# Emitting the engine programs without a Block, with the final waits shared between ScalarE and SyncE

## The chip, the cores and the metric

The kernel runs on one core of a Trainium2 chip. The metric is the device time of one execution in microseconds (us). The core has five engines that run their own instruction streams and meet only at semaphores: TensorE (PE in the profile), VectorE (DVE), ScalarE (ACT), GpSimd (POOL) and SyncE (SP), which here only issues transfers (DMAs) and waits.

## What is computed

One input `x` of 2048 tokens by 640 features is normalised, and two branches of the normalised `xn` are added to it: a linear attention with 32 heads of 20 features, and a dense layer with GELU.

```python
def _A_ref(x, wqkv, wo):
    H = 32; Dh = D // H
    qkv = (x @ wqkv).reshape(B, S, 3, H, Dh).transpose(2, 0, 3, 1, 4)
    q, k, v = qkv[0], qkv[1], qkv[2]
    phi = lambda t: jnp.where(t > 0, t + 1, jnp.exp(t)) + 1e-6
    pq, pk = phi(q), phi(k)
    kv = jnp.einsum("bhsd,bhse->bhde", pk, v)
    z = jnp.einsum("bhsd->bhd", pk)
    num = jnp.einsum("bhqd,bhde->bhqe", pq, kv)
    den = jnp.einsum("bhqd,bhd->bhq", pq, z)[..., None] + 1e-6
    return (num / den).transpose(0, 2, 1, 3).reshape(B, S, D) @ wo

def _B_ref(x, w1, b1, w2, b2):
    return jnp.einsum("bsf,fd->bsd", _gelu(jnp.einsum("bsd,df->bsf", x, w1) + b1), w2) + b2

xn = _layernorm(x, axis=-1)
return x + _A_ref(xn, A_wqkv, A_wo) + _B_ref(xn, B_w1, B_b1, B_w2, B_b2)
```

All inputs and the output are bf16; F, the width of the dense layer, is 1536.

## The kernel before

The 2048 tokens are cut into 16 tiles of 128 (`t`), in 4 chunks of 4 (`c`). In order of time, TensorE does this: transposes and the first dense layer (lines 382 and 352) with GELU on ScalarE; the keys of all tiles (line 473); the product of `phi(k)` with `xn`, summed over all tokens (line 512); the queries (line 524), with the small products that fold values and `wo` into one matrix `Msb` (lines 533 and 551) and the denominators (line 562) among them; and then, per token tile, the second dense layer and the attention's output in one accumulation (line 615). The last tile is done in three column parts of 320, 192 and 128 (line 651).

VectorE adds the residual to each finished tile (line 634; the last tile's parts at line 654) and writes a small buffer `out_sb`. SyncE then issues the store to the output (line 637; parts at line 657). In the same last stage SyncE also copies the reciprocals of the denominators to all partitions (`rden_dma`, line 586: four transfers for each of four chunks). ScalarE has no work in that stage after the five copies into `Msb` at line 556, and GpSimd none after the memset at line 480.

The order of the work is written out by hand. A small class `Planner` records it: `ins` appends an instruction to the list of its engine with the semaphore values that it has to wait for, and remembers per engine what has already been waited for. Each DMA has a semaphore of its own, complete at 16. `wait_event` appends a record that has waits and no instruction. `emit` goes through the five lists, in the order TensorE, VectorE, ScalarE, GpSimd, SyncE, and puts out every wait (line 94) ahead of its instruction; waits that are left at the end of a list go out at line 108.

At the end (lines 683 to 692) the kernel before lets SyncE wait for the last three records of its own list, which are the stores of the three parts, and emits each engine's list into a block of its own inside `nc.Block()`. Closing that block emits the instructions that the profile has at line 691: a drain on every engine, then a barrier in which GpSimd collects the other four and releases them. An opening barrier, line 706, comes with the making of the program and is no part of the block.

The head of the kernel is touched only in that it too is no longer inside a block. There SyncE loads the tokens and most of the weights (lines 229 and 233), and ScalarE, ahead of its first activation (line 392, with a load of the activation table), issues two loads (line 233): the bias `b1` and the first quarter of `W1`, which TensorE needs at line 382.

Of the kernel before, what the change touches and what calls it, by code (L numbers as in the profile page):

```python
# [23 lines left out]
class Planner:  # L24
# [55 lines left out]
    def emit(self, block):  # L80
        nc = self.nc
        for idx, eng_name in enumerate(ENGINES):
            recs = self.records[eng_name]
            if not recs:
                continue

            def body(eng, recs=recs, eng_name=eng_name):
                pending_waits = []
                for (waits, fns, ev, dma) in recs:
                    pending_waits.extend(waits)  # L90
                    if not fns:
                        continue
                    for (key, val) in pending_waits:
                        eng.wait_ge(self.sems[key], val)
                    pending_waits = []
                    ins = None
                    for fn in fns:
                        r = fn(eng)
                        if r is not None:
                            ins = r  # L100
                    if ev is not None:
                        key, val = ev
                        if dma:
                            ins.then_inc(self.sems[key], 16)
                        else:
                            ins.then_inc(self.sems[eng_name], 1)
                for (key, val) in pending_waits:
                    eng.wait_ge(self.sems[key], val)

            getattr(block, eng_name)(body)  # L110


def bass_parallel_sum__linear_attn_block__dense_activation_gelu__prompt_kernel(
# [16 lines left out]
    Pl = Planner(nc)  # L130
# [6 lines left out]
    with contextlib.ExitStack() as es:  # L137
# [45 lines left out]
        def take(n):  # L183
            b = ring[0]
            if n == 2 and b % 2:
                b += 1
            b %= 8
            ring[0] = (b + n) % 8
            return b
# [278 lines left out]
        for t in range(NT):  # L468
            b = take(2)
            fns = []  # L470
# [142 lines left out]
        def mm(b, t, i, h):  # L613
            l, r = mm_ops(t, i)
            return lambda e: e.matmul(bank(b + h, 0, HW), l, r[:, h * HW:(h + 1) * HW],  # L615
                                      start=(i == 0), stop=(i == JT + DT - 1))

        def mm_reads(t, i):
            return [r_HG[t][i], r_W2] if i < JT else [r_PQ[t // CH][i - JT]] + r_M[i - JT]

        def out_w2(t, lo=0, hi=JT, b=None):
            b = take(2) if b is None else b
            for i in range(lo, hi):
                Pl.ins("tensor", [mm(b, t, i, 0), mm(b, t, i, 1)], reads=mm_reads(t, i), writes=B_[b:b + 2],
                       mark=(i == JT - 1))
            return b
# [13 lines left out]
        def out_last(t):  # L640
            xb(t)
            lo = 0
            for i, w in enumerate((HW, 3 * 64, P)):
# [5 lines left out]
                for q in range(JT + DT):  # L649
# [7 lines left out]
                Pl.ins("sync", lambda e, hs=hs, o=o: e.dma_start(ov[t * P:(t + 1) * P, hs], o),  # L657
                       reads=[r_out3 if i == 2 else r_out[i]], dma=True)

        bs = [out_w2(0)]  # L660
        bs += [(bs[0] + 2 * i) % 8 for i in range(1, 4)]
        m_step(bs[1:4])
# [17 lines left out]
                rden_dma({4: 2, 7: 3}[t])  # L680
        out_last(NT - 1)

        for (waits, fns, ev, dma) in Pl.records["sync"][-3:]:
            Pl.wait_event("sync", ev)

        with contextlib.ExitStack() as ses:
            for e_ in ENGINES:
                Pl.sems[e_] = ses.enter_context(nc.semaphore(f"s_{e_}"))
            for i in range(Pl.ndma):
                Pl.sems[f"dma{i}"] = ses.enter_context(nc.semaphore(f"s_dma{i}"))  # L690
            with nc.allow_low_precision("bf16 operands as in the reference"), nc.Block() as block:
                Pl.emit(block)


# [26 lines left out]
```

## Time and profile before

| | |
|---|---|
| median of three timed runs | 209.23 us (209.12 to 209.23) |
| the profiled execution, its own time | 208.79 us |
| its span, first to last instruction of the program | 207.0 us |
| TensorE busy | 203.1 us (98%) |
| VectorE, ScalarE, GpSimd busy | 112.3, 73.2, 21.2 us |
| output stores of a whole tile, issue to landing | 1.8 us |
| stores of the last three parts, issue to landing | 1.6, 1.5, 1.4 us |
| clock granted to TensorE | 1.00 |

The span counts everything that the program itself issues, waits and barriers among it. Waits, barriers, branches and the issuing of transfers are done by an engine's sequencer and are not counted as busy. They carry a "q" behind the engine's name (SPq, POOLq; PEld is TensorE's loading of weights). A transfer's time to landing runs from its issue to the arrival of its semaphore. The profiled execution is one, and its own time lies somewhat below the median of the timed runs.

### The profile page before, as it was taken

The numbers are of one execution on the slowest core, as the hardware profiler recorded it, in microseconds if no ns is written. First come the engines' busy times: TensorE is split into PE (matmuls) and PEld (weight loads), VectorE is DVE, ScalarE is ACT, GpSimd is POOL, SyncE is SP. The second block draws the span as 40 slices with busy tenths as digits, with TensorE's granted clock in tenths as the row PEclk, the third lists the DMA queues.
The fourth block names the chain that finished last, engine by engine and source line by source line (L and its number), as shares of the span: only waits on it lengthen the run. The fifth ranks groups of instructions, "written<-read, shape, count | busy, mean of one in ns | idle before, by whom it ended". The sixth has DMA issues, their size and how long they took to land.

```text
span 207.0 us, 3957 instructions
## 1 busy us (share of the span) xinstructions
PE 203.1 (98%) x1588; PEld 140.4 (68%) x1588; DVE 112.3 (54%) x231; ACT 73.2 (35%) x141; POOL 21.2 (10%) x59
## 2 busy tenths in 40 slices
PE   7999999999999999999999999999999999999995
PEld 2799987444457777777756556777777777777775
DVE  4589970000007888999298887564863422523322
ACT  2689887666676455111153553400000000000000
POOL 3235568000031000000000000000000000000000
DMA  6999678997000000000300001921212111001001
GB/s 180 345 354 103 106 131 149 372 324 263 3 0 0 0 0 3 0 3 0 63 0 5 0 0 48 375 96 44 88 42 69 53 38 54 32 32 36 32 33 62
DMA packets 24042, 18.31 MB, mean 88 GB/s; under 512 B 10584, under 2 KB 24024, under 8 KB 24024
## 3 DMA queue, kind: packets, MB, share of 16 engines
q1 hardware_dynamic: 23344, 17.57, 29.8%
q10 hardware_dynamic: 680, 0.49, 0.8%
q8 instruction: 12, 0.20, 0.4%
q14 instruction: 6, 0.05, 0.1%
HBM read 12.62 MB, written 2.62 MB: 74 GB/s over the span
## 4 chain that ended last, share of the span: by engine, by line
PE 96%; DMA 3%; ACTq 0%; DVE 0%; issue 0%
PE ps L615 34%; PE ps L352 25%; PE ps L512 10%; PE ps L473 10%; PE ps L524 10%; DMA W<-in_B_w_dram 3%; PE ps L651 2%; PE ps L551 1%; PE ps L533 1%; PE ps L562 1%; PE ps L382 0%; PE ps L336 0%; ACTq L233 0%; DVE out_sb L654 0%
## 5 line engine op out<-in xcount | busy, mean ns | idle before, releaser
L352 PE MATMUL ps<-xnT,W 128*128 128x128 bf16 (+2 forms) x435 | 52.0, 282 | 0.0
L615 PE MATMUL ps<-W,HG 128*128 128x320 bf16 x360 | 51.0, 299 | 0.0
L352 PEld LDWEIGHTS ps<-xnT,W 128*128 128x128 bf16 x435 | 35.6, 98 | 15.6
L615 PEld LDWEIGHTS ps<-W,HG 128*128 128x128 bf16 x360 | 35.1, 98 | 14.2 <-issue 0.4
L356 ACT ACTIVATE HG<-ps,b1c 128x128 bf16<-128x128 f32 (+2 forms) x87 | 40.0, 493 | 12.4 <-PE ps L352 10.3
L460 ACT ACTIVATE ek<-ps 128x512 bf16<-128x512 f32 (+1 forms) x36 | 23.2, 645 | 20.3 <-PE ps L524 10.6
L634 DVE TENSOR_TENSOR out_sb<-ps,xnT 128x640 bf16<-128x640 f32 x15 | 12.4, 825 | 33.1 <-PE ps L615 32.9
L461 DVE TENSOR_SCALAR ek<-ek 128x512 bf16<-128x512 bf16 (+1 forms) x36 | 10.9, 303 | 33.7 <-ACT ek L460 32.5
L615 PE MATMUL ps<-Msb,PQ 128*128 128x320 bf16 x150 | 22.3, 299 | 0.0
L524 PE MATMUL ps<-xnT,Wqkv 128*128 128x512 bf16 x100 | 21.9, 379 | 0.0
L473 PE MATMUL ps<-Wqkv,xnT 128*128 128x320 bf16 x160 | 21.9, 299 | 0.0
L512 PE MATMUL ps<-xPK,xn_tm 128*128 128x320 bf16 x160 | 21.9, 299 | 0.0
L473 PEld LDWEIGHTS ps<-Wqkv,xnT 128*128 128x128 bf16 x160 | 15.7, 98 | 6.2
L512 PEld LDWEIGHTS ps<-xPK,xn_tm 128*128 128x128 bf16 x160 | 15.7, 98 | 6.1
L615 PEld LDWEIGHTS ps<-Msb,PQ 128*128 128x128 bf16 x150 | 14.7, 98 | 5.7
L524 PEld LDWEIGHTS ps<-xnT,Wqkv 128*128 128x128 bf16 x100 | 11.7, 117 | 9.5
L463 DVE SCALAR_TENSOR_TENSOR PQ<-ps,ek 128x512 bf16<-128x512 f32 x20 | 13.8, 692 | 2.1
L308 DVE BATCH_NORM_STATS2 stats<-xPK 128x6 f32<-128x320 bf16 x32 | 13.6, 466 | 2.4 <-DMA xPK<-in_A_x_dram 2.3
L463 DVE SCALAR_TENSOR_TENSOR xPK<-ps,ek 128x640 bf16<-128x640 f32 x16 | 13.2, 825 | 1.7
L499 DVE TENSOR_TENSOR Msb<-Msb,xPK 128x640 f32<-128x640 f32 x14 | 11.6, 825 | 0.5
L318 POOL TENSOR_TENSOR rstd<-aggr,mhalf 128x1 f32<-128x1 f32 x16 | 9.1, 569 | 8.9 <-DVE aggr L316 8.9
L516 ACT ACTIVATE W<-ps 128x640 bf16<-128x640 f32 x5 | 3.5, 705 | 18.2 <-PE ps L512 18.2
(61 smaller groups left out, 93.6 us busy)
## 6 DMA issues: line engine op xcount, KB each, us to landing
xnT<-in_A_x_dram SPq DMA_DIRECT2D x4, 640.0 KB, 6.2
Wqkv<-in_A_wqkv_dram SPq DMA_DIRECT2D x3, 800.0 KB, 6.5
out_dram<-out_sb SPq DMA_DIRECT2D x15, 160.0 KB, 1.8
W<-in_B_w_dram SPq DMA_DIRECT2D x1, 1920.0 KB, 15.9
W<-in_B_w_dram SPq DMA_DIRECT2D x3, 480.0 KB, 7.0
xPK<-in_A_x_dram SPq DMA_DIRECT2D x2, 640.0 KB, 8.7
Wo<-in_A_wo_dram SPq DMA_DIRECT2D x1, 800.0 KB, 11.3
xPK<-in_A_x_dram SPq DMA_DIRECT2D x4, 160.0 KB, 4.2
```

Source lines behind the costliest of these rows:

```text
L308: Pl.ins(v, lambda e: e.bn_stats(stats[:, s, 6 * h:6 * h + 6], x_in[:, t, h * HW:(h + 1) * HW]), reads=[r_x[t]], writes=[r_stats[s][h]])
L352: Pl.ins("tensor", [(lambda e, k=k: e.matmul(bank(b, 0, w), W1[:, k, jb * P:(jb + 1) * P], xnT[:, k, tok], start=(k == 0), stop=(k == DT - ...
L356: Pl.ins("scalar", lambda e: e.activation(HG[:, jb, tok], bank(b, 0, w), ACT.Gelu_apprx_tanh, bias=b1c[:, jb:jb + 1]), reads=[B_[b], r_b1c ...
L460: Pl.ins("scalar", lambda e: e.activation(e2, src, ACT.Exp), reads=br, writes=[r_ek[s]])
L461: Pl.ins(v, lambda e: e.tensor_scalar(et, et, 1.0, 1e-6, ALU.min, ALU.add), reads=[r_ek[s]], writes=[r_ek[s]])
L463: Pl.ins(v, lambda e: e.scalar_tensor_tensor(out=d2, in0=src, scalar=0.0, in1=e2, op0=ALU.max, op1=ALU.add), reads=br + [r_ek[s]], writes= ...
L473: fns.append(lambda e, k=k, h=h, b=b, t=t: e.matmul(bank(b + h, 0, HW), xnT[:, k, t * P:(t + 1) * P], Wqkv[:, k, D + h * HW:D + (h + 1) * ...
L499: Pl.ins(v, lambda e, t=t: e.tensor_tensor(out=zsum, in0=zsum, in1=PK[:, t, :], op=ALU.add), reads=[r_PK[t], r_zsum], writes=[r_zsum])
L512: Pl.ins("tensor", [(lambda e, t=t, h=h, b=b, f=f: e.matmul(bank(b + h, 0, HW), xn_tm[:, t, f * P:(f + 1) * P], PK[:, t, h * HW:(h + 1) * ...
L524: Pl.ins("tensor", [(lambda e, k=k, j=j, b=b: e.matmul(bank(b), Wqkv[:, k, j:D:DT], xnT[:, k, cc], start=(k == 0), stop=(k == DT - 1))) fo ...
L615: return lambda e: e.matmul(bank(b + h, 0, HW), l, r[:, h * HW:(h + 1) * HW], start=(i == 0), stop=(i == JT + DT - 1))
L634: Pl.ins(v, lambda e: e.tensor_tensor(out=halves(out_sb[:, s, :]), in0=pair(b), in1=halves(x_res[:, t, :]), op=ALU.add), reads=B_[b:b + 2] ...
```

## The change

The engine lists are emitted one after the other straight into the main program, where before each went into a block. `nc.Block()` and what its closing emits are gone. The final waits are other ones: all DMAs that SyncE issues from `n_sync` on, which is set after the queries and the four reloads of `x`, are gathered in `stores` (the copies of `rden`, the stores of 15 tiles and of the three parts). ScalarE waits for all of these but the last, at the end of its own list; SyncE waits for the last one.

```diff
@@ emit
-            getattr(block, eng_name)(body)
+            body(getattr(nc, eng_name))
@@ kernel function
+        n_sync = len(Pl.records["sync"])
         bs = [out_w2(0)]
...
         out_last(NT - 1)
 
-        for (waits, fns, ev, dma) in Pl.records["sync"][-3:]:
-            Pl.wait_event("sync", ev)
+        stores = [ev for (waits, fns, ev, dma) in Pl.records["sync"][n_sync:] if dma]
+        for ev in stores[:-1]:
+            Pl.wait_event("scalar", ev)
+        Pl.wait_event("sync", stores[-1])
...
-            with nc.allow_low_precision("bf16 operands as in the reference"), nc.Block() as block:
-                Pl.emit(block)
+            with nc.allow_low_precision("bf16 operands as in the reference"):
+                Pl.emit(None)
```

## The prediction

> **What bounds the kernel now.** I read the page's first line and busy shares, then the chain that ended last, then its end in order of time, then SyncE's own waits, and last every instruction of the closing barrier (line 691).
>
> The page and its chain:
> ```profile
> span 207.0 us, 3957 instructions
> PE 203.1 (98%) x1588; PEld 140.4 (68%) x1588; DVE 112.3 (54%) x231; ACT 73.2 (35%) x141; POOL 21.2 (10%) x59
> ...
> PE 96%; DMA 3%; ACTq 0%; DVE 0%; issue 0%
> ```
> TensorE is busy in 98% of the span and carries 96% of the chain. Nothing this diff touches lies in that stretch. The other 3% is one transfer at the start, the first quarter of W1. The chain in order of time has it, and the end:
> ```profile
> 0.80 0.62 ACTq L233
> 1.42 0.04 issue
> 1.45 5.34 DMA W<-in_B_w_dram
> ...
> 6.83 1.01 PE ps L382 x15
> ...
> 200.09 4.67 PE ps L651 x51
> 204.77 0.02 issue
> 204.79 0.29 DVE out_sb L654
> ```
> The chain counts compute only and stops at 204.79 + 0.29 = 205.08 us; the span goes on to 207.03. So 1.95 us of the span lie behind the last compute instruction: the last store, and the program's end. SyncE's own waits and the closing barrier's instructions show them:
> ```profile
> SPq L108 <- DMA out_dram<-out_sb: 1.1, 1, 1.1
> ...
> SPq L691 <- PEq L691: 0.2, 1, 0.2
> ```
> ```profile
> L691 POOLq EVENT_SEMAPHORE  x2: 17/17/17, 206.8 to 206.9; - x2
> ...
> L691 PEldq DRAIN  x1: 1222/1222/1222, 203.6 to 203.6; - x1
> L691 DVEq DRAIN  x1: 330/330/330, 204.8 to 204.8; - x1
> L691 SPq COMPARE_BRANCH  x1: 41/41/41, 206.6 to 206.6; - x1
> L691 SPq DRAIN  x1: 13/13/13, 206.8 to 206.8; - x1
> L691 SPq EVENT_SEMAPHORE  x1: 17/17/17, 207.0 to 207.0; - x1
> ...
> L691 PEldq EVENT_SEMAPHORE  x1: 51/51/51, 207.0 to 207.0; - x1
> ```
> The view rounds starts to 0.1 us; the trace's records hold nanoseconds. By them the last store is issued at 205.112 and lands at 206.554. SyncE's wait for two of the three stores (line 108) runs 206.571 to 206.599, the branch that leaves its block and carries the third wait 206.636 to 206.677, its drain 206.809 to 206.822, GpSimd collects at 206.847 and releases at 206.930 to 206.947, and the engines leave between 206.971 (SyncE) and 207.034 (TensorE, 51 ns). The end is bound by the last store and then by 207.034 - 206.554 = 0.48 us of waiting and barrier.
>
> **What the Trainium skill says.** (1) "Runtime: NRT & Kernel Launch", section "The ~15µs preamble/postamble breakdown": the runtime puts its own barrier behind the kernel, about 1.5 us that wait for all engines, and a hop of such a chain through the engines costs 44 ns. The profile shows nothing of this: the run took 208.79 us against a span of 207.03, and the 1.76 us outside carry no label. They are less than the sum of the page's stages, so only part of these can be in the time. (2) The same page, "Instruction fetch mechanics": a taken branch whose target isn't in the current window forces a fetch. SyncE's branch is followed by a hole of 206.809 - 206.677 = 0.132 us ahead of its drain, against 0.037 us between its wait and the branch; it fits, without showing the cause. (3) "Perfetto Trace Analysis", section "DMA Instruction — HWDGE (DVE, Sync)": a transfer's semaphore comes after its write is confirmed, which can take surprisingly long to HBM. The trace agrees: 32 KB take 1.44 us from issue to landing, and the change leaves that wait where it is.
>
> **The change, part by part.**
>
> *The end on SyncE.* Removed: the branch with its fetch hole, the drain, the two GpSimd steps and the five releases. Kept: one wait for the last store. I take it at the row of line 108, starting 17 ns behind the landing and taking 28 ns: 206.571 to 206.599. The three waits become one, but the first two had been satisfied at 204.996 and 205.716, so only the third ever counted. The span should end at 206.60: a gain of 207.034 - 206.599 = 0.435 us. Bounds: at most 0.48, if the wait itself cost nothing; at least 0.435 - 0.078 - 0.145 = 0.21 us, if a branch and a drain of the same cost still follow the wait (206.599 to 206.677, then 206.677 to 206.822).
>
> *The other engines' ends.* Their drains go too. TensorE's runs over the last matmuls, DVE's over the last add, ScalarE's is done at 133.42 and GpSimd's at 63.15; all are over by 205.14, 1.4 us ahead of the landing. Worth nothing: the store covers them, and were that cover gone DVE's 0.33 us would be the price.
>
> *ScalarE's new waits.* `stores` holds every DMA that SyncE issues after `n_sync`: 16 copies of rden (line 586), 15 output stores (line 637) and 3 parts (line 657), 34 in all. ScalarE waits for the first 33. Its last activation ends at 133.38 and nothing of it is queued behind the waits, so they hold up nobody; no engine waits for ScalarE after line 556. A wait instruction on ScalarE takes 17 to 38 ns (line 94), so even 33 of them, with the 0.06 us gap SyncE shows between such waits, come to 33 x 0.10 = 3.3 us of its 73 us of idleness. They are met as the stores land, in the order of issue. The last is for the second part, landed at 205.716; with one more wait of 0.1 us ScalarE is through at about 205.82, and SyncE only at 206.60. Cost nothing, with 0.78 us to spare; without that cover, the last wait's 0.1 us.
>
> *The start.* No branch into a block is recorded: from the opening barrier (line 706) to the first work are 0.066 us on SyncE and 0.056 on ScalarE, and 0.058 between SyncE's first two transfers. The gain is between 0 and 0.03 us; I take 0. No DMA changes its queue or place, and no buffer comes free at another time.
>
> *Behind the span.* Before, all five engines leave within 63 ns of each other. After, four have left long ago when SyncE ends, and may have done their share of the runtime's barrier. The trace shows none of it. One bound is 0; the other an estimate from the runtime page: of a chain up and down five engines the four hops up can be done ahead, 4 x 0.044 = 0.18 us. I take the middle, 0.09.
>
> *Sum.* Against the profiled execution: 208.79 - 0.435 - 0.09 = 208.27 us. The three timed runs have a median of 209.23, 0.44 longer than that execution; none of the terms depends on what sets them apart, so from the median: 209.23 - 0.53 = 208.70 us. TensorE is what is late next: it ends at 204.77, and add, store and landing follow.
>
> **The rivals.** *R1, the forecast:* the barrier goes and nothing replaces it, 208.70, with 208.54 (0.48 + 0.03 + 0.18 gained) to 208.80 (0.435 gained) for its own bounds apart from noise. For it: every step removed stands behind the last landing in the records.
>
> *R2, something takes its place.* The main program ends with a branch and drain of its own (gain 0.21 and no more, 209.02), or what follows outside the span has a start-up of its own on SyncE, a fetch for instance, which the 0.48 us used to hide (gain near 0, up to 209.23). For it: 1.76 us outside the span that no record explains, and a hole of 0.13 us at the only branch. Against it: SyncE did not reach its end early before; its fetch could run ahead of the barrier only by the last 0.48 us. I put it at 209.08, between its two forms.
>
> *R3, slower: ScalarE's first load is issued later.* W1's first quarter goes out on ScalarE's queue at 1.452, after b1, and holds TensorE until 6.83. The activation table load of line 392 (1.283 us) stands behind that issue now. If the straight program put it ahead, W1 would land 1.28 us later; PE is nearly gapless from there, so all of it would reach the end: 209.23 + 1.28 - 0.53 = 209.98. It decides from 0.53 us of delay, where it eats the gain. Against it: the table load has the line of the first activation and stands just before it though the block begins two issues earlier, so it goes with the activation and not with the block's head.
>
> **How the numbers follow.** About 0.2% (0.42 us) is what a measurement of this kernel can tell from no change. R1's middle, a gain of 0.53, is only just beyond it; its low bound, 0.435, sits on it, so noise can carry it to either side. R1 has 0.68, of which 0.58 fall faster and 0.10 same. R2 has 0.22: 0.21 same, 0.01 slower by noise. R3 and other shifts at the start have 0.10, slower. So faster 0.58, same 0.31, slower 0.11. The timed runs differ by 0.11 us, and the profiled one by 0.44, so the range has to reach past R1's own: down to 208.35, R1's best with a little of that spread, and up to 209.20, which takes in nearly all of R2 and leaves out R3. R1's own range with the noise is 208.40 to 208.95.
>
> **What would show it.** Right: no record of line 691 at all, SyncE's last instruction a wait that starts some 17 ns after the last landing and ends the span, about 1.5 us behind the last add; ScalarE with some 17 to 33 waits after 133.4, the last before 206; first matmul of line 382 still at 6.8; time outside the span 1.7 us. Wrong: a branch or drain behind SyncE's wait, or an outside part of over 2.1 us (R2); a table load ahead of ScalarE's first transfers and line 382 later than 7.3 (R3). If the outside part is the same to 0.02 us, the 0.09 was nothing and the gain is 0.44.

## The result and the profile after

The changed kernel takes 208.17 us (median of six runs, 207.96 to 208.50) against 209.18 us for the kernel before (six runs, 208.82 to 209.55). The ratio is 0.9953 with a 95% interval of 0.9940 to 0.9967: faster by 0.5%, or 1.01 us by the medians. The forecast was 208.70, a gain of 0.53, and its range reached down to 208.35.

First, the kernel after: the page's first two lines, and SyncE's own waits from 195 us on (who waited for whom, us in total, times, longest).

```profile
span 206.8 us, 3962 instructions
PE 203.2 (98%) x1588; PEld 140.3 (68%) x1588; DVE 112.3 (54%) x231; ACT 73.1 (35%) x141; POOL 21.1 (10%) x59
```
```profile
SPq L637 <- DVE out_sb L634: 8.5, 2, 4.3
SPq L657 <- DVE out_sb L654: 3.1, 3, 2.1
SPq L108 <- DMA out_dram<-out_sb: 1.1, 1, 1.1
```

The wait for the barrier (line 691) is gone; the wait for the last store stands as it did, 1.1 us. The waits at line 108 in the kernel after (engine, operation, count; shortest, median and longest in ns; first and last start):

```profile
L108 ACTq EVENT_SEMAPHORE  x17: 17/38/38, 159.1 to 205.9; - x17
L108 SPq EVENT_SEMAPHORE  x1: 17/17/17, 206.8 to 206.8; - x1
```

ScalarE's 33 waits became 17 instructions. The last starts at 205.935, and SyncE's wait runs from 206.750 to 206.767 and ends the span. The last store lands at 206.733, so from landing to the end of the span it is now 0.034 us, where it was 0.480: 0.45 us gained there. The chain of the kernel after, its start and its end:

```profile
1.45 5.37 DMA W<-in_B_w_dram
...
6.87 1.01 PE ps L382 x15
...
8.16 3.65 PE ps L352 x55
11.82 0.37 PE ps L336 x5
...
200.28 4.67 PE ps L651 x51
204.95 0.02 issue
204.97 0.29 DVE out_sb L654
```

The start is as it was: W1's first quarter goes out at 1.45 and TensorE takes it up at 6.87. In this one execution the last compute lies 0.18 us later than in the one before (204.97 against 204.79): 0.04 from line 382's start, 0.09 from the five transposes at 11.82, 0.05 from the matmuls ahead of them. All of that lies in the first 12 us, where TensorE still depends on loads: the transposes wait 0.20 us for `xn_tm` there, and VectorE, ahead of making it, waited 0.65 us for a load of tokens where it had waited 0.44. Such differences come without any change to the head of the program: in the profiled executions of the experiments below, line 382 starts anywhere from 6.58 to 7.47 us at the full granted clock. The span is therefore only 207.034 - 206.767 = 0.27 us shorter (0.45 - 0.18).

The rest is outside. The profiled execution took 208.04 us, so 208.04 - 206.767 = 1.27 us lie outside its span, against 1.76 before. Over the six runs after, the difference of time and span (spans to 0.1 us) is 1.20 to 1.28 us, median 1.24. Some six tenths of the gain (0.48 of 0.75 us between the two profiled executions) are in time that no instruction of the program occupies. No record shows how this time is divided between what lies ahead of the span's first instruction and what lies behind its last. That the end is what differs follows only from the experiments, where kernels that differ in their final waits alone differ outside.

### The profile page after: what moved, and what is told of

It is laid out like the page before. It is cut to its first block, busy times and chain, and to the rows that moved or that the text cites. A ratio compares the mean times of both kernels' runs of the same rounds, so it can differ in the third digit from the quotient of the medians.

```text
span 206.8 us, 3962 instructions
## 1 busy us (share of the span) xinstructions
PE 203.2 (98%) x1588; PEld 140.3 (68%) x1588; DVE 112.3 (54%) x231; ACT 73.1 (35%) x141; POOL 21.1 (10%) x59
## 4 chain that ended last, share of the span: by engine, by line
PE 96%; DMA 3%; ACTq 0%; DVE 0%; issue 0%
PE ps L615 34%; PE ps L352 25%; PE ps L473 11%; PE ps L512 11%; PE ps L524 10%; DMA W<-in_B_w_dram 3%; PE ps L651 2%; PE ps L551 1%; PE ps L533 1%; PE ps L562 1%; PE ps L382 0%; PE ps L336 0%; ACTq L233 0%; DVE out_sb L654 0%
```

## The experiments

All kernels give the whole computation. Each was timed over several executions with the kernel before on the same chip. "Outside" is time less span, as a median over the kernel's timed executions; "landing to end" is, in the profiled one, its time less the moment, counted from the span's start, at which the last store lands. Both leave out the start, whose differences blur the whole times. The kernel before was measured again with each group (e1 to e4, e5, e6): 209.32, 209.31 and 209.27 us, outside 1.90, 1.95 and 1.89 (lowest 1.70, highest 2.08). The table's row for it has the time of the result and the outside part of the last group. Two of the profiled executions (e3_straight_barrier and e5_last_pe) had a granted clock of 0.992 and are 2 us longer than the medians of their kernels; of them only what follows the last landing is used.

| kernel | us | ratio to before (95%) | outside | landing to end |
|---|---|---|---|---|
| before | 209.18 | | 1.89 | 2.24 |
| after | 208.17 | 0.9953 (0.9940 to 0.9967) | 1.24 | 1.31 |
| e1_straight_old_waits | 208.37 | 0.9955 (0.9938 to 0.9973) | 1.30 | 1.36 |
| e2_block_new_waits | 209.11 | 0.9990 (0.9971 to 1.0009) | 1.74 | 2.13 |
| e3_straight_barrier | 208.85 | 0.9985 (0.9973 to 0.9998) | 1.74 | 2.02 |
| e4_all_wait_last | 208.79 | 0.9982 (0.9963 to 1.0001) | 1.73 | 1.85 |
| e5_last_pe | 208.46 | 0.9958 (0.9942 to 0.9973) | 1.57 | 1.64 |
| e5_last_dve | 208.44 | 0.9967 (0.9937 to 0.9997) | 1.39 | 1.45 |
| e5_last_act | 208.40 | 0.9959 (0.9949 to 0.9969) | 1.59 | 1.57 |
| e5_last_pool | 208.73 | 0.9970 (0.9961 to 0.9980) | 1.83 | 1.88 |
| e6_block_both_waits | 209.06 | 0.9988 (0.9969 to 1.0007) | 1.74 | 2.23 |
| e6_all_but_pool | 208.62 | 0.9967 (0.9953 to 0.9982) | 1.52 | 1.61 |
| e6_pool_second | 208.15 | 0.9942 (0.9923 to 0.9962) | 1.26 | 1.31 |
| e6_pool_part_late | 208.47 | 0.9955 (0.9942 to 0.9969) | 1.57 | 1.56 |

### Blocks, barrier or waits

*e1_straight_old_waits.* The straight program with the old final waits:
```diff
-        for ev in stores[:-1]:
-            Pl.wait_event("scalar", ev)
-        Pl.wait_event("sync", stores[-1])
+        for (waits, fns, ev, dma) in Pl.records["sync"][-3:]:
+            Pl.wait_event("sync", ev)
```


> The straight program, but with the final waits of before: SyncE waits for the three parts' stores, ScalarE for nothing. The time outside the span was 1.76 us before and 1.24 after. Theory A (four engines that leave early do their share of what follows ahead of SyncE, so it is the arrival together that costs): outside 1.2 to 1.3 us, and the span as after, some 0.4 us below before; in all 1.0 us below before. Theory B (the blocks, with their branches and the layout of the program, cost the time outside the span): the same numbers. Theory C (it is the split of the waits, ScalarE idling at the end until a short time before SyncE): outside 1.7 us, only 0.4 us below before.

1.30 us outside and a ratio of 0.9955: with none of ScalarE's waits, nearly the whole gain is there. Theory C falls. The three waits on SyncE cost next to nothing beside the one: in the profile of this kernel they are two instructions, the second ending 0.045 us behind the landing (after: 0.034).

```profile
L108 SPq EVENT_SEMAPHORE  x2: 17/22/28, 206.4 to 207.2; - x2
```

*e2_block_new_waits.* The kernel before, with the waits of after in place of its own; the mirror of the first.

> The Block and its closing barrier of before, with the final waits of after (33 on ScalarE, one on SyncE). Theories A and B: outside 1.76 us, span within 0.1 us of before, so no difference. Theory C: outside 1.2 to 1.3 us, 0.5 us below before.

Outside 1.74 us, and the ratio's interval holds 1. Theories A and B stand; C falls a second time. That 1.74 is below the 1.90 of before on the same chip was expected by none of them; e6_block_both_waits takes it up.

*e3_straight_barrier.* The kernel after, with a barrier by hand:
```diff
                 Pl.emit(None)
+                nc.all_engine_barrier()
```


> The straight program of after with one barrier of all engines put at its end, with no block and no branch. Theory A: outside 1.7 to 1.8 us as before, since all engines leave together; the span about 0.35 us longer than after; in all within 0.2 us of before. Theory B: outside 1.2 to 1.3 us, so some 0.5 us below before.

No block and no branch, and yet 1.74 us outside: theory B falls, theory A is met. The whole time is not within 0.2 us of before, as expected, but 0.3 below it by the ratio: the barrier is shorter in the span than the Block's, and outside, too, 1.74 stands against 1.90, as in e2_block_new_waits. The barrier itself, in the profile of this kernel:

```profile
L696 POOLq EVENT_SEMAPHORE  x2: 17/17/17, 209.0 to 209.1; - x2
...
L696 SPq DRAIN  x1: 13/13/13, 209.0 to 209.0; - x1
L696 SPq EVENT_SEMAPHORE  x1: 17/17/17, 209.1 to 209.1; - x1
...
L696 PEldq EVENT_SEMAPHORE  x1: 51/51/51, 209.1 to 209.1; - x1
```
From the last landing (208.886) to the span's end (209.177) it takes 0.29 us, against 0.48 with the Block. Of the 0.19 between them, 0.17 are the branch with its hole: here the drain follows SyncE's wait after 0.037 us, where in the Block 0.210 pass (206.599 to 206.809).

*e4_all_wait_last.* No barrier; all five engines wait for the last store:
```diff
         Pl.wait_event("sync", stores[-1])
+        for e_ in ("tensor", "vector", "scalar", "gpsimd"):
+            Pl.wait_event(e_, stores[-1])
```


> The straight program of after, but TensorE, VectorE, ScalarE and GpSimd wait for the last store too, each with a wait of its own and no barrier. The span is that of after, or 0.05 us more for the slowest wait. Theory A: outside 1.7 to 1.8 us, since all five leave together; in all 0.4 us below before. Theory B, and a third, D (the drains and the barrier's own instructions delay what follows): outside 1.2 to 1.3 us, as after, 0.9 to 1.0 us below before.

```profile
L108 ACTq EVENT_SEMAPHORE  x17: 38/38/38, 161.6 to 207.0; - x17
L108 SPq EVENT_SEMAPHORE  x1: 17/17/17, 206.9 to 206.9; - x1
L108 POOLq EVENT_SEMAPHORE  x1: 17/17/17, 207.0 to 207.0; - x1
L108 DVEq EVENT_SEMAPHORE  x1: 21/21/21, 207.0 to 207.0; - x1
L108 PEldq EVENT_SEMAPHORE  x1: 51/51/51, 207.0 to 207.0; - x1
```
The engines end their last waits within 0.05 us of each other (206.966 to 207.012), with no drain and no barrier at the end, and outside is 1.73 us. Theory D falls with B: it is enough that all engines leave late.

### Which engine

In the next four, SyncE waits for the first 33 transfers and one other engine for the last store:
```diff
         for ev in stores[:-1]:
-            Pl.wait_event("scalar", ev)
-        Pl.wait_event("sync", stores[-1])
+            Pl.wait_event("sync", ev)
+        Pl.wait_event("gpsimd", stores[-1])
```
with "tensor", "vector" or "scalar" for "gpsimd" in the others.

> The straight program with the waits dealt out anew: SyncE waits for the first 33 transfers and is through some 0.8 us before the end, TensorE alone waits for the last store, the other three end early. With all five waiting the time outside the span was 1.73 us, with SyncE alone 1.24. Theory A1 (one engine has the longest way out, and the time outside is that of whichever late engine has the longest): one of the four engines alone gives 1.7, the others 1.2 to 1.3 or less. Theory A2 (the engines pass on one after the other, so every early engine saves a step): each of the four alone gives something between, 1.1 to 1.6, by its place in the order, and none gives 1.73. For TensorE, whose wait instruction is the slowest (51 ns): A1 1.7, A2 1.3.

> The same, with VectorE alone waiting for the last store. A1: outside 1.2 to 1.3 us unless VectorE is the one with the long way out (then 1.7). A2: 1.1 to 1.6.

> The same, with ScalarE alone waiting for the last store. A1: outside 1.2 to 1.3 us unless ScalarE is the one with the long way out (then 1.7). A2: 1.1 to 1.6.

> The same, with GpSimd alone waiting for the last store. A1: outside 1.2 to 1.3 us unless GpSimd is the one with the long way out (then 1.7). A2: 1.1 to 1.6.

One thing in the set-up was wrong: SyncE comes to its waits only behind the issue of the last store, and they take a microsecond. In the profile with GpSimd last:

```profile
L108 SPq EVENT_SEMAPHORE  x15: 17/28/28, 206.0 to 206.8; - x15
L108 POOLq EVENT_SEMAPHORE  x1: 17/17/17, 207.1 to 207.1; - x1
```
SyncE is through only 0.2 us ahead of the last engine, not 0.8. By the measure of after it would end the run 1.24 us behind its own last wait, some 0.4 to 0.8 us ahead of the times measured in all four, so it does not decide them.

Outside is 1.83 us with GpSimd last, 1.59 with ScalarE, 1.57 with TensorE, 1.39 with VectorE, against 1.24 with SyncE (the kernel after). GpSimd has the long way out, as A1 said, but the others are not alike, as A1 had it, and GpSimd alone costs all that five engines cost, which A2 excluded. What fits all is a mended A1: every engine has its own time from its last instruction to the end of the run, and the run ends with the latest of these sums. With e4_all_wait_last: GpSimd's wait ends at 206.974, and 206.974 + 1.83 = 208.80 against 208.78 measured. With e3_straight_barrier: 209.090 + 1.83 = 210.92 against 210.91. With the kernel before: 206.947 + 1.83 = 208.78 against 208.79. But this execution of the kernel before, with 1.76 us outside, is among those with the least there. GpSimd's sum gives 1.74 us outside for it, and the medians of 1.89 to 1.95 lie 0.15 to 0.21 above that; e6_block_both_waits takes this up.

### The sum put to the test

*e6_all_but_pool.* As e4_all_wait_last, without GpSimd's wait.

> The straight program; TensorE, VectorE, ScalarE and SyncE wait for the last store, GpSimd alone leaves early. With all five waiting it was 1.73 us outside, with one alone waiting GpSimd 1.83, ScalarE 1.59, TensorE 1.57, VectorE 1.39, SyncE 1.24. Theory A1 (the end is the latest of the engines' ends plus each one's own way out): TensorE decides, 1.52 to 1.6 us. Theory H (GpSimd's share is an additional step of its own, so that without it the sum of four others still counts): 1.65 or more. A further one, that it is the number of late engines: 1.7.

1.52 us, within 0.05 us of what TensorE gives alone (1.57); by TensorE's sum, 207.369 + 1.57 = 208.94 against 208.90 measured. Theory H and the count of late engines fall.

*e6_pool_second* and *e6_pool_part_late*: the kernel after, with GpSimd brought nearer to the end in two steps.
```diff
         Pl.wait_event("sync", stores[-1])
+        Pl.wait_event("gpsimd", stores[-2])
+        ev = Pl.ins(g, lambda e: e.memset(warm[:], 0.0), writes=[r_warm])
+        Pl.wait_event("gpsimd", ev)
```
(The first has the first added line only.)

> The kernel after, with one wait more: GpSimd waits for the store of the last tile's second part, which lands 0.82 us ahead of the last one. Theory A1: GpSimd's end, 0.8 us ahead, plus 1.83 is earlier than SyncE's end plus 1.24, so nothing changes: outside 1.2 to 1.3 us. Were it enough for GpSimd to have been idle long before (it is at its end from 63 us on in the kernel after), then 1.5 to 1.8.

> As the kernel before it in this series, but after its wait GpSimd also fills a 128x512 tile that nobody reads any more, and waits for that, so that it ends some 0.2 to 0.35 us ahead of SyncE instead of 0.8. Theory A1: outside = 1.83 less that lead, 1.5 to 1.65 us. A theory by which an engine that comes ahead of the last one at all costs nothing: 1.24.

In the first kernel, GpSimd's wait and SyncE's are

```profile
L108 POOLq EVENT_SEMAPHORE  x1: 17/17/17, 205.9 to 205.9; - x1
L108 SPq EVENT_SEMAPHORE  x1: 17/17/17, 206.8 to 206.8; - x1
```
With GpSimd at its end 0.8 us ahead of SyncE nothing changes: 1.26 us. With the fill in between, GpSimd's waits and the fill in the second kernel are

```profile
L689 POOL MEMSET warm<- x1: 524/524/524, 205.7 to 205.7; 128x512 bf16 x1
```
```profile
L108 POOLq EVENT_SEMAPHORE  x1: 17/17/17, 206.3 to 206.3; - x1
L108 SPq EVENT_SEMAPHORE  x1: 17/17/17, 206.5 to 206.5; - x1
```
GpSimd ends at 206.308, 0.25 us ahead of SyncE (206.556). The sum gives 1.83 - 0.25 = 1.58; measured are 1.57 as a median and 1.52 in the profiled execution. By the sum, a lead is worth its own length until GpSimd no longer decides, at 1.83 - 1.24 = 0.59 us; the leads of 0.25 and 0.8 us agree with it. The second kernel has a fill on GpSimd beside its shorter lead, and no run has the fill with a long lead; that the lead counts and not the fill rests on the size, which the sum foretold.

*e6_block_both_waits.* The kernel before; ScalarE gets the waits of after in addition:
```diff
+        n_sync = len(Pl.records["sync"])
...
+        for ev in stores[:-1]:
+            Pl.wait_event("scalar", ev)
         for ev in stores[-3:]:
             Pl.wait_event("sync", ev)
```


> The Block, its barrier and SyncE's three waits as before; added are only ScalarE's 33 waits of after, ahead of the barrier. With the waits dealt out as after, the Block had 1.74 us outside the span, and before itself 1.90 on the same chip. Theory F (before, the page of instructions that ScalarE needs for its way out is fetched only behind the barrier, at 208.75 in the profile, and the waits bring it forward to 172): outside 1.74, narrow, and no late fetch. Theory G (SyncE's own three waits or their place cost it): outside 1.9 as before.

Outside is 1.74 us (1.67 to 1.80), with before at 1.89 (1.74 to 2.07): theory F is met in its number, G falls. The trace's records of instruction loads have, for the kernel before, one of 8 KB at 208.75, behind the barrier; here, as in the kernel after, a load of 8 KB comes among ScalarE's waits instead, at 172.9 (after: 172.1). The page counts these loads by queue, without the late one, first for the kernel before and then for this one:

```profile
q14 instruction: 6, 0.05, 0.1%
```
```profile
q14 instruction: 7, 0.06, 0.1%
```
That ScalarE's waits take 0.15 us off the Block's time outside is shown; that the earlier load is the reason is not. For it: of the other kernels only e5_last_act has such a load late, at 208.26, and there, too, the time outside varies widely (1.39 to 1.75 us). Against it: counted from the span's start, the late load ends at 209.09 in the kernel before and at 208.68 in e5_last_act, in both 0.30 us behind the measured time (208.79 and 208.38). So either the end of the execution doesn't wait for this load, or the measured time doesn't begin with the span. In the straight program ScalarE's waits make little difference: e1_straight_old_waits, where ScalarE's last activation ends at 134 us, has 1.30.

## Why the prediction was wrong

*The end on SyncE*: right. Forecast 0.435 us, measured 0.480 - 0.034 = 0.45, near the upper bound of 0.48, since the single wait takes 17 ns and not the 28 of a double one. No branch and no drain follows it. The branch with the hole behind it is worth 0.17 us (0.210 against 0.037 from the wait to the drain). For the hole the prediction drew on the Trainium skill, "Runtime: NRT & Kernel Launch", section "Instruction fetch mechanics", by which a taken branch to a target outside the window has to fetch it. The trace doesn't show such a fetch: the kernel before has no instruction load on record between 189.15 and 208.75 us, and the hole lies at 206.68 to 206.81. What fills it is open.

*The other engines' ends*: the drains cost nothing inside the span, as said. But the step looked only at their durations and not at what each engine still has to do behind them. This is where the failed step below has its root.

*ScalarE's new waits*: they cost nothing, as said; 205.97 was their end, for an estimate of 205.82. Within the kernel after they also bring next to nothing (1.24 against 1.30 outside).

*The start*: right. W1's load is issued at 1.45 as before and rival R3, the table load moved ahead, did not occur (it still starts at 1.89).

*Behind the span*: this step failed, in its size. I put 0.09 us on it, at most 0.18, from the 44 ns that the Trainium skill gives for a hop of a barrier through the engines ("Runtime: NRT & Kernel Launch", section "The ~15µs preamble/postamble breakdown"). Measured is 1.76 - 1.27 = 0.48 between the two profiled executions and 1.89 - 1.24 = 0.65 by the medians. The larger part, 1.74 - 1.24 = 0.50, comes from the mechanism named: four engines are done ahead of SyncE. But their worth is not so many hops: the barrier held GpSimd, whose way out is 1.83 us, until the others were there, and now SyncE alone ends late, whose way out is the shortest, 1.24. The other 0.15 is what goes away when ScalarE has its waits ahead of the Block's barrier (e6_block_both_waits); no step had it, and its cause is open. No instruction in the profile shows either; only the 1.76 us without a label said that there was room, and the upper bound should have been drawn from it and not from the hop.

The sum: 0.45 + 0.65 = 1.10 against 1.01 measured by the medians; the remainder is within the spread of the start, which alone moved the two profiled executions 0.18 us apart.

Of the rivals, R2 (something takes the place of the barrier, or what follows has a start-up on SyncE that it used to hide) had the sign of the unseen part wrong. Its form, that the time outside the span depends on how the program ends, was true.

What stays open: of what the ways out consist. Each was measured as time less span, so what lies ahead of the span is in all five, and their differences are surer than their lengths. Their order, from GpSimd with 1.83 down to SyncE with 1.24, would also come from a chain through the engines that begins with GpSimd and ends with SyncE; then each would take up its step from the one before. The runs here give only the sums. Open, too, is the 0.15 us that go with ScalarE's waits.

## What to carry to other kernels

This kernel ends in a wait for a store, and there a closing barrier of all engines cost twice: its own instructions behind the landing (0.29 us, 0.48 with the block's branch), and the late leaving of engines that could have been gone (0.5 us). Let each engine run out as soon as its own work is done, and let the engine with the shortest way out, here SyncE, hold the last wait. Time outside the span is not a constant: take the difference of time and span before and after, and give it a bound as wide as the part that has no label.

## What the runs showed of the hardware

The time outside the span depends on the engine that ends last: 1.24 us with SyncE, 1.39 with VectorE, 1.57 with TensorE, 1.59 with ScalarE (1.39 to 1.75 from run to run, where the others vary by 0.1), 1.83 with GpSimd. GpSimd, idle from 63 us on in the kernel before, was thus held by the barrier to an end that accounts for 1.74 of that kernel's 1.89 us outside. A taken branch at the end of SyncE's stream cost some 0.17 us more than none (0.210 against 0.037 us from the wait to the drain), with no instruction load on record in its hole.
